# Moving two portions of an attention product from one step of a nine-step cycle to the step before it

## The chip, the cores and the metric

The kernel runs on one core of one Trainium2 chip. The metric is the time of one execution on the device, in microseconds. Each time before is one of 3 runs, and their median is what the change is compared with.

## What is computed

Attention over 8 batches and 8 heads, 576 positions, head size 64, with scores that lie more than tau below their row's largest dropped; then a mixture of 8 experts with one expert for each token. Cut to what matters:

```python
scores = scale * np.matmul(q, k.transpose(0, 1, 3, 2))
thresh = np.max(scores, axis=-1, keepdims=True) - tau
scores = np.where(scores >= thresh, scores, -1000000000.0)
attn = np.exp(scores - np.max(scores, axis=-1, keepdims=True))
attn = attn / (np.sum(attn, axis=-1, keepdims=True) + 1e-09)
x = np.matmul(attn, v)            # then tokens x (heads * head_dim)
e_idx = np.argmax(x @ w_gate, axis=1)
h = np.maximum(x[mask] @ w1[e], 0.0)
out[mask] = gate_w[mask, None] * eom[mask, e, None] * (h @ w2[e])
```

## The kernel before, in words

The attention comes first and takes about half of the span; the experts follow. The order of the instructions on TensorE (PE), VectorE (DVE), ScalarE (ACT) and GpSimd (POOL) is the order in which the code issues them. Only the DMA queue of SyncE (SP) gets its order from a scheduler.

A **unit** u is one head of two batches, which lie on the two halves of the 128 partitions; there are 32 units. Two units make a **pair** m, 16 pairs in all (0 to 15), and a pair is worked off in nine **steps** s = 0 to 8. `Attention.at` says what a step's scores are: steps 0 to 3 the four 128-row tiles of the even unit, step 4 the 64 remaining rows of both units, steps 5 to 8 the four tiles of the odd unit. The loop of `Attention.run` counts steps as g = 9 m + s, and a tile goes through it in three steps:

- In step g, `scores` multiplies q and k on TensorE into two PSUM buffers named `ps` (line L142), one for each batch. Their pool `ps_s` (L62) has two buffers in all, so the scores of the next step can be written only where this step's have been read. VectorE reads them with one operation for each batch (L153), which writes scaled scores `s` and their smallest value. ScalarE takes the exponential into `p` (`exps`, L171).
- In step g + 1, `masks` (L183, VectorE) multiplies `p` by the mask in two operations. In VectorE's queue the two masks of the tile before stand behind the two score operations of the tile now.
- In step g + 2, TensorE transposes `p`: the 64 last columns by `remainder` (L206), into a corner of the PSUM buffers `pa` or `pr`, or into fresh ones (`spots` chooses), and the rest by `blocks` (L238) into `pt`. ScalarE copies both to SBUF (L212, L241, L244), into `PTa` (the first 256 rows) and `PTb` (the last 320).

The product with the values, `av_units`, is done when a unit's tiles are transposed. It is a generator of nine **portions**: four with `PTa` into `pa`, one for the last 64 keys, and four with `PTb` into `pr` (all L252). One of the last four is two matmuls of 320 columns, which the profile shows as 4 records. After the fifth and the ninth portion the result is to be copied to `X` by ScalarE (L264 and L271); `close` issues that copy. The table `AV` (L28) says for each step which unit's portions are issued and how many, with the unit counted from 2 m. In `run` they come between the step's scores and its transposes. In step 4 (`SPLIT`) ScalarE's two exponentials stand one ahead of the transposes' corner copies and one behind.

In steps 1 and 5 (`ROWS`) `x_rows` (L306) turns a finished `X` into rows of tokens and router logits, through fresh `pr` and `pa`; in step 5 that is the odd unit of the pair before, whose product the changed entries of `AV` issue. The pairs 5 to 15 also carry operations of the router on VectorE, GpSimd and TensorE.

Of the kernel before, what the change touches and what calls it, by code (L numbers as in the profile page):

```python
# [20 lines left out]
class Attention:  # L21
# [3 lines left out]
    LB = 3  # L25
    VB = 4
    WARM = {0: 4, 1: 2}
    AV = {0: (-2, 2), 2: (-1, 5), 3: (-1, 2), 4: (-1, 2), 6: (0, 3), 7: (0, 2), 8: (0, 2)}  # L28
    SPLIT = (0, 4, 7)
    ROWS = {1: -2, 5: -1}  # L30
    LOGITS = {3: -2, 7: -1}
# [304 lines left out]
    def run(self, hooks):  # L336
# [4 lines left out]
        for g in range(G + self.TAIL):  # L341
# [36 lines left out]
            if not soon:  # L378
                self.exps(g, st, pr, (0,) if split else (0, 1))
            if s in self.AV:  # L380
                du, n = self.AV[s]
                au = 2 * m + du
# [975 lines left out]
```

## Time and profile before

| what | us |
|---|---|
| median of 3 runs | 906.42 |
| lowest and highest of them | 906.08, 906.98 |
| the profiled execution, its own time | 904.05 |
| span of that execution (first to last instruction) | 902.3 |
| busy in the span: PE, DVE, ACT, POOL | 891.8, 683.2, 595.6, 388.7 |

The profiled execution is 2.37 us (0.26%) below the median. A row of a timeline gives an instruction's start in microseconds from the start of the span, its duration, engine, line, operation, output and inputs, and, in brackets, how long the engine had been idle before it and what ended that. Durations overlap their successors a little on every engine, so the length of a piece of work is read here from start to start. Equal matmuls are merged into one row; the "x8" of one is its number of records, and a float32 matmul leaves two.

### The profile page before, as it was taken

The page shows a single profiled execution, that of the slowest core. Times are in us where ns is not written, and L with a number is a line of the kernel's source. Part 1 is how long each engine was busy: PE and PEld are TensorE (multiplying, and loading weights), DVE is VectorE, ACT ScalarE, POOL GpSimd, SP SyncE. Part 2 cuts the span into 40 slices and gives each one's busy share as a digit, 9 for nine tenths or more (in the row PEclk, how much of TensorE's full clock was granted, in tenths as well). Part 3 has the DMA queues.
Part 4 walks back from the last instruction along what each step waited for, and adds up shares of the span by engine and source line. Part 5 has one row for each costly group of instructions (what it writes and reads, how often), then busy time and mean ns, then how long its engine had stood idle before and what let it go on. Part 6 is the DMA issues. An engine that isn't in the chain of part 4 may idle for free. (4 is left out here: it accounts for less than half of the span.)

```text
span 902.3 us, 22172 instructions
## 1 busy us (share of the span) xinstructions
PE 891.8 (99%) x8345; PEld 680.5 (75%) x8345; DVE 683.2 (76%) x1704; ACT 595.6 (66%) x1159; POOL 388.7 (43%) x673
## 2 busy tenths in 40 slices
PE   8999999999999999999999999999999999999996
PEld 4666666666666666666678899888998888998885
DVE  7999999999999999999977775656556446456631
ACT  6899989999899998999974443335435335345521
POOL 4456656667866677668756710202102101112001
PEclk9999999999999999999999999999999999999999
DMA  5287421222512224254226993437646436647301
GB/s 173 93 270 235 142 87 45 85 75 79 168 44 86 73 82 165 93 170 147 96 74 204 315 293 96 152 100 241 198 143 200 162 119 213 205 128 248 114 13 45
DMA packets 70117, 127.88 MB, mean 142 GB/s; under 512 B 6408, under 2 KB 33288, under 8 KB 70009
## 3 DMA queue, kind: packets, MB, share of 16 engines
q1 hardware_dynamic: 63465, 106.03, 37.1%
q0 software_dynamic: 6544, 20.42, 5.9%
q8 instruction: 66, 1.08, 0.5%
q14 instruction: 42, 0.34, 0.1%
HBM read 95.26 MB, written 31.86 MB: 141 GB/s over the span
## 5 line engine op out<-in xcount | busy, mean ns | idle before, releaser
L171 ACT ACTIVATE p<-s,mn 128x576 f32<-128x576 f32 x288 | 215.7, 797 | 32.5 <-DVE s L153 32.5
L183 DVE SCALAR_TENSOR_TENSOR p<-s,thr,p 128x576 f32<-128x576 f32 x288 | 228.0, 828 | 3.0 <-POOL thr L160 2.8
L153 DVE TENSOR_SCALAR_CACHE_REDUCE s<-ps 128x576 f32<-128x576 f32 x288 | 206.1, 751 | 16.9 <-PE ps L142 16.5
L849 POOL DMA_INDIRECT out_dram<-yo,kid x39 | 46.4, 1189 | 323.0 <-DVE yo L848 216.7
L142 PE MATMUL ps<-qk 64*128 64x288 f32 (+1 forms) x1280 | 182.2, 419 | 0.0
L1053 ACT ACTIVATE hh<-ph 128x256 fp32r<-128x256 f32 (+7 forms) x103 | 48.7, 473 | 182.6 <-PE ph L1051 182.5
L160 POOL TENSOR_SCALAR thr<-mn,tau_sb 128x2 f32<-128x2 f32 x144 | 98.6, 685 | 129.8 <-DVE s L153 126.8
L1051 PE MATMUL ph<-xh,w1h 128*128 128x256 f32 (+7 forms) x412 | 136.7, 332 | 0.0
L1051 PE MATMUL ph<-xh,w1l 128*128 128x256 f32 (+7 forms) x412 | 133.5, 325 | 0.0
L1054 DVE SCALAR_TENSOR_TENSOR hl<-ph,hh 128x256 fp32r<-128x256 f32 (+7 forms) x103 | 54.4, 529 | 103.9 <-ACT hh L1053 103.7
L1051 PE MATMUL ph<-xl,w1h 128*128 128x256 f32 (+7 forms) x412 | 132.3, 326 | 0.0
L142 PEld LDWEIGHTS ps<-qk 64*128 64x128 f32 (+1 forms) x1280 | 108.3, 177 | 17.6 <-DVE s L153 2.8
L252 PE MATMUL pr<-PTb,vld 128*64 128x320 f32 (+1 forms) x640 | 107.2, 447 | 0.0
L238 PE MATMUL pt<-ident,p 64*128 64x64 f32 x2288 | 95.1, 223 | 0.3
L252 PE MATMUL pa<-PTa,vld 128*64 128x256 f32 (+1 forms) x640 | 84.6, 391 | 0.0
L1071 PE MATMUL py<-w2h,hh 128*128 128x512 f32 (+3 forms) x213 | 84.2, 395 | 0.0
L1072 PE MATMUL py<-w2l,hh 128*128 128x512 f32 (+3 forms) x213 | 84.0, 394 | 0.0
L1073 PE MATMUL py<-w2h,hl 128*128 128x512 f32 (+3 forms) x213 | 84.0, 394 | 0.0
L238 PEld LDWEIGHTS pt<-ident,p 64*128 64x128 f32 x2288 | 82.5, 138 | 0.8 <-ACT PTa L241 0.5
L1051 PEld LDWEIGHTS ph<-xh,w1h 128*128 128x128 f32 x412 | 77.4, 188 | 7.3
L1051 PEld LDWEIGHTS ph<-xl,w1h 128*128 128x128 f32 x412 | 77.0, 188 | 5.8
L1051 PEld LDWEIGHTS ph<-xh,w1l 128*128 128x128 f32 x412 | 77.5, 188 | 4.3
(206 smaller groups left out, 1636.9 us busy)
## 6 DMA issues: line engine op xcount, KB each, us to landing
r<-in_moe_w_dram SPq DMA_DIRECT2D x104, 512.0 KB, 3.9
qk<-in_qkv_dram SPq DMA_DIRECT2D x31, 608.0 KB, 3.9
xs<-zrow SPq DMA_DIRECT2D x40, 257.0 KB, 4.3
vld<-in_qkv_dram SPq DMA_DIRECT2D x32, 320.0 KB, 3.9
xg<-xs SPq DMA_DIRECT2D x4, 771.0 KB, 6.2
xg<-xs SPq DMA_DIRECT2D x6, 514.0 KB, 4.5
xg<-xs SPq DMA_DIRECT2D x3, 1028.0 KB, 8.3
xg<-xs SPq DMA_DIRECT2D x6, 128.5 KB, 8.3
```

Source lines behind the costliest of these rows:

```text
L142: nc.tensor.matmul(ps[a][rows, o : o + HS], q[pp, t * P : t * P + w], k[pp, k0 : k0 + HS], start=True, stop=True)
L153: nc.vector.tensor_scalar(s, ps[a][:, c0 : c0 + S], SC, None, op0=ALU.mult, op1=ALU.min, accum_out=mn[:, a : a + 1])
L160: self.router.gate = nc.gpsimd.tensor_scalar(thr, mn, self.tau, None, op0=ALU.add)
L171: self.nc.scalar.activation(e, ss[a], AF.Exp, bias=mn[:, a : a + 1], scale=-1.0)
L183: nc.vector.scalar_tensor_tensor(e, s, thr[:, a : a + 1], e, op0=ALU.is_le, op1=ALU.mult, accum_out=acc[:, a ^ (t > 1) : (a ^ (t > 1)) + 1])
L238: nc.tensor.transpose(pt[:, o : o + 64], p[hs[h], k0 : k0 + P], id_[hs[h], hs[h]])
L252: one = lambda out, l, r, start, stop: nc.tensor.matmul(out, l, r, start=start, stop=stop, skip_group_check=True)
L1051: nc.tensor.matmul(ph, w[:, c, fs], x[:, c, 0:N], start=(i == 0), stop=(i == 11))
L1054: nc.vector.scalar_tensor_tensor(hl[:, 0:N], ph, 0.0, hh[:, 0:N], op0=ALU.max, op1=ALU.subtract)
L1071: nc.tensor.matmul(Y, hh[:, ts], wh, start=(f == 0), stop=False)
L1072: nc.tensor.matmul(Y, hh[:, ts], wl, start=False, stop=False)
L1073: nc.tensor.matmul(Y, hl[:, ts], wh, start=False, stop=(f == 7))
```

## The change

The entry of step 3 goes from 2 portions to 4, and the entry of step 4 is taken out. Nothing else in the code is touched.

```diff
-    AV = {0: (-2, 2), 2: (-1, 5), 3: (-1, 2), 4: (-1, 2), 6: (0, 3), 7: (0, 2), 8: (0, 2)}
+    AV = {0: (-2, 2), 2: (-1, 5), 3: (-1, 4), 6: (0, 3), 7: (0, 2), 8: (0, 2)}
```

The product of a pair's odd unit is done in steps 2 to 4 of the next pair, so the change moves instructions in pairs 1 to 15; in pair 0 these steps have no products. Behind pair 15 the entries also serve unit 31, but no scores stand between them there, and TensorE's order is the same with both tables.

On TensorE, steps 3 and 4 of a pair without router work, before (`ps` scores, `pr<-PTb` products, `ident` transposes):

```order
L142 MATMUL ps<-qk 128x288 x4
L252 MATMUL pr<-PTb,vld 64x320 x4
L206 MATMUL pa<-ident,p 128x64
L206 MATMUL pr<-ident,p 128x64
L238 MATMUL pt<-ident,p 128x64 x16
L142 MATMUL ps<-qk 64x288 x8
L252 MATMUL pr<-PTb,vld 64x320 x4
L206 MATMUL pa<-ident,p 128x64
L206 MATMUL pr<-ident,p 128x64
L238 MATMUL pt<-ident,p 128x64 x16
L142 MATMUL ps<-qk 128x288 x4
```

and the same two steps with the change:

```order
L142 MATMUL ps<-qk 128x288 x4
L252 MATMUL pr<-PTb,vld 64x320 x8
L206 MATMUL pa<-ident,p 128x64
L206 MATMUL pr<-ident,p 128x64
L238 MATMUL pt<-ident,p 128x64 x16
L142 MATMUL ps<-qk 64x288 x8
L206 MATMUL pa<-ident,p 128x64
L206 MATMUL pr<-ident,p 128x64
L238 MATMUL pt<-ident,p 128x64 x16
L142 MATMUL ps<-qk 128x288 x4
```

Four matmuls of 320 columns went from between the scores and the transposes of step 4 to the same place of step 3. In step 4 the transposes now follow the scores directly, and their corner is a fresh `pr`.

On ScalarE, the same steps before (`X` is the copy of the product; the first four rows belong to step 3, the others to step 4):

```order
L171 ACTIVATE p<-s,mn 128x576 x2
L212 COPY PTa<-pa 128x64
L212 COPY PTa<-pr 128x64
L241 COPY PTa<-pt 128x8x128
L171 ACTIVATE p<-s,mn 128x576
L271 COPY X_215<-pr 128x320
L212 COPY PTb<-pa 128x64
```

and with the change:

```order
L171 ACTIVATE p<-s,mn 128x576 x2
L271 COPY X_215<-pr 128x320
L212 COPY PTa<-pa 128x64
L212 COPY PTa<-pr 128x64
L241 COPY PTa<-pt 128x8x128
L171 ACTIVATE p<-s,mn 128x576
L212 COPY PTb<-pa 128x64
```

The copy of the finished product moved with its last portion, from step 4 to step 3. VectorE's and GpSimd's orders are the same as before. On SP the loads of q and k and of v, which alternated, now mostly stand in twos:

```order
L96 DMA qk<-in_qkv_dram 128x1216 x2
L101 DMA vld<-in_qkv_dram 128x640 x2
```

so a load of q and k can stand behind a load of v that it stood ahead of.

## Rows read from the trace of the kernel before

**Rows 1.** Stretches from:to, with length, busy time (instructions) by engine, clock, DMA.

```profile
60.00:115.60 55.60, 55.60 (x726) 36.45 (x724) 52.42 (x148) 50.89 (x109) 33.52 (x52) 1.00 0.62 202
...
470.00:880.00 410.00, 410.00 (x2423) 362.85 (x2423) 238.63 (x450) 174.34 (x275) 80.67 (x92) 1.00 0.54 174
```

**Rows 2.** Timeline of TensorE, pair 3, steps 3 to 6: start, us, instructions.

```profile
96.46 1.19 PE L142 MATMUL ps<-qk 64*128 64x288 f32 x8
97.58 1.30 PE L252 MATMUL pr<-PTb,vld 128*64 128x320 f32 x8
...
99.51 1.20 PE L142 MATMUL ps<-qk 64*64 64x288 f32 x16
100.64 1.30 PE L252 MATMUL pr<-PTb,vld 128*64 128x320 f32 x8
101.86 0.27 PE L206 MATMUL pa<-ident,p 64*128 64x64 f32 x1
...
102.48 1.19 PE L142 MATMUL ps<-qk 64*128 64x288 f32 x8
103.50 0.23 PE L306 MATMUL pa<-wx,X 64*128 64x80 f32 x1
...
105.14 1.30 PE L142 MATMUL ps<-qk 64*128 64x288 f32 x8
106.36 1.51 PE L252 MATMUL pa<-PTa,vld 128*64 128x256 f32 x12
```

**Rows 3.** Timeline of VectorE, pair 3, steps 2 to 8, and of step 0 after.

```profile
93.45 0.75 DVE L153 TENSOR_SCALAR_CACHE_REDUCE s<-ps 128x576 f32<-128x576 f32 x1
...
97.68 0.76 DVE L153 TENSOR_SCALAR_CACHE_REDUCE s<-ps 128x576 f32<-128x576 f32 x1 [1.18 <-PE ps L142]
...
100.78 0.76 DVE L153 TENSOR_SCALAR_CACHE_REDUCE s<-ps 128x576 f32<-128x576 f32 x1 [0.18 <-PE ps L142]
...
103.70 0.76 DVE L153 TENSOR_SCALAR_CACHE_REDUCE s<-ps 128x576 f32<-128x576 f32 x1
...
104.39 0.75 DVE L153 TENSOR_SCALAR_CACHE_REDUCE s<-ps 128x576 f32<-128x576 f32 x1
...
106.54 0.75 DVE L153 TENSOR_SCALAR_CACHE_REDUCE s<-ps 128x576 f32<-128x576 f32 x1
...
109.64 0.76 DVE L153 TENSOR_SCALAR_CACHE_REDUCE s<-ps 128x576 f32<-128x576 f32 x1 [0.17 <-PE ps L142]
...
115.61 0.76 DVE L153 TENSOR_SCALAR_CACHE_REDUCE s<-ps 128x576 f32<-128x576 f32 x1
```

**Rows 4.** Timeline of VectorE, pair 0, steps 3 to 5, which have no products.

```profile
14.18 0.75 DVE L153 TENSOR_SCALAR_CACHE_REDUCE s<-ps 128x576 f32<-128x576 f32 x1
...
15.54 0.81 DVE L183 SCALAR_TENSOR_TENSOR p<-s,thr,p 128x576 f32<-128x576 f32 x1
...
17.02 0.75 DVE L153 TENSOR_SCALAR_CACHE_REDUCE s<-ps 128x576 f32<-128x576 f32 x1
...
19.85 0.75 DVE L153 TENSOR_SCALAR_CACHE_REDUCE s<-ps 128x576 f32<-128x576 f32 x1
```

**Rows 5.** Timeline of SyncE: the load of the q and k used first in Rows 6.

```profile
84.95 0.40 SPq L96 DMA_DIRECT2D qk<-in_qkv_dram  x1
```

**Rows 6.** Timeline of TensorE: the first scores of pair 4.

```profile
114.38 1.19 PE L142 MATMUL ps<-qk 64*128 64x288 f32 x8
```

**Rows 7.** Tile qk from 60 to 440 us: its loads to their landing.

```profile
DMA to landing us min/median/max: 3.6/3.8/6.6
```

**Rows 8.** Timeline of ScalarE, pair 3, from step 4 to step 6.

```profile
101.58 0.78 ACT L171 ACTIVATE p<-s,mn 128x576 f32<-128x576 f32 x1 [0.52 <-DVE s L153]
102.27 0.41 ACT L271 COPY X<-pr 128x320 f32<-128x320 f32 x1
...
104.92 0.49 ACT L363 COPY xl<-pa 128x400 f32<-128x400 f32 x1 [0.44 <-PE pa L206]
...
108.15 0.24 ACT L212 COPY PTb<-pa 128x64 f32<-128x64 f32 x1
```

## The prediction

> **What bounds the kernel now.** I read the stretches first. In the undisturbed part of the attention (60 to 115.6 us) TensorE is shown busy all the time and VectorE for 52.42 of 55.60 us; among the experts TensorE is busy all the time and VectorE for 238.63 of 410 us [rows 1]. So the experts follow TensorE's own work, which the change leaves as it is, and what the attention loses or gains moves the end by as much. In the attention two engines are close to full, and which one sets the time must be read step by step.
>
> For that I took the timelines of one cycle, pair 3. On TensorE step 3 lasts from 96.46 to 99.51, 3.05 us, and step 4 to 102.48, 2.97 us; step 5 then lasts 2.66 us [rows 2]. On VectorE I take the starts of each step's first score operation: 93.45, 97.68, 100.78, 103.70, 106.54 for steps 2 to 6 [rows 3]. Steps 2 to 5 thus last 4.23, 3.10, 2.92 and 2.84 us. Ahead of step 3 VectorE waits 1.18 us for scores, because step 2 has five portions; ahead of step 4 it waits 0.18 us [rows 3]. So TensorE paces steps 2 and 3.
>
> What VectorE needs for a step by itself is seen in pair 0, whose steps 3 and 4 have no products: from first score operation to first score operation 17.02 - 14.18 = 2.84 and 19.85 - 17.02 = 2.83 us. Two score operations take 15.54 - 14.18 = 1.36 us of that, and two masks the other 1.48 [rows 4]. Step 5 of pair 3 is at this floor; step 4 is 0.08 above it. A cycle lasts the sum of its steps, each at the slower of the two engines, so long as neither can run ahead.
>
> **Can one run ahead?** Hardly. VectorE's score operations of step 4 need TensorE's scores of step 4, which stand behind all products of step 3. VectorE cannot fill the wait with masks, since its masks of the next tile stand behind those score operations in its queue. TensorE cannot run ahead either, because the two `ps` buffers hold one step's scores: those of step 5 go where VectorE has read those of step 4. So what a long step loses on VectorE, a short step on TensorE does not give back.
>
> **The change part by part.**
>
> Step 3 gains two portions. In step 4 they take 101.86 - 100.64 = 1.22 us [rows 2], and in step 3 they stand between scores and transposes as there. TensorE's step 3 becomes 3.05 + 1.22 = 4.27 us, and VectorE's interval 3.10 + 1.22 = 4.32 us. VectorE's wait ahead of step 4 grows from 0.18 to about 1.4 us. Nothing hides it: +1.22.
>
> Step 4 loses them. TensorE's own work in it falls to 2.97 - 1.22 = 1.75 us. But its scores reach VectorE 100.78 - 99.51 = 1.27 us after the step begins [rows 2, 3], and from there VectorE needs its 2.84 us to the next first score operation [rows 4]. The interval goes from 2.92 to 2.84: -0.08. On TensorE the wait appears at the scores of step 5. They are ready to start 1.75 us into step 4, and the first `ps` is free at 1.27 + 0.76 = 2.03 us, the second at about 1.27 + 0.69 + 0.75 = 2.71 us (103.70 and 104.39 give the 0.69) [rows 3]. About 1 us of idle time or stretched scores replaces the products.
>
> Does TensorE keep a lead afterwards? Step 5 is at VectorE's floor already. The scores of step 6 wait for the second `ps` in the kernel before too: they start at 105.14, when the second score operation of step 5 ends (104.39 + 0.75), and take 106.36 - 105.14 = 1.22 us, against 97.58 - 96.46 = 1.12 in step 3 [rows 2, 3]. An earlier step 5 on TensorE can take out those 0.10 us and no more. I set this gain to zero, the value of the kernel before, and keep 0.10 for the range.
>
> The copy of `X` moves from step 4 to step 3 on ScalarE. Ahead of the exponential of step 4 ScalarE was idle for 0.52 us [rows 8], and step 3 gets 1.22 us longer, so the copy of 0.41 us is covered; without that cover it would cost at most itself. The fresh `pr` of step 4's corner needs that copy done. It comes right behind the last portion, more than a step's scores ahead of its use: nothing.
>
> The loads that change places on SP: q and k for pair 4 were issued at 84.95 [rows 5], a load lands within 6.6 us at most [rows 7], and the first scores with them start at 114.38 [rows 6]. That leaves 114.38 - 84.95 - 6.6 = 22.8 us for a load of v ahead in the queue: nothing. Without that cover, the price would be the 3.8 us of a landing at each late load.
>
> The sum: 1.22 - 0.08 = +1.14 us for a pair, in 15 pairs: **+17.1 us**. With the 0.10 of step 6 it is 1.04 x 15 = 15.6; where step 4 is not shortened at all, 1.22 x 15 = 18.3. Pairs with router work have longer steps 4 on VectorE that do not shrink, which goes towards the upper end. The profiled execution would go from 904.05 to 921.2. It lies 2.37 us under the median, so against the median of 906.42 the forecast is **923.5 us**, with 922.0 to 924.7 from these bounds.
>
> **The rivals.**
>
> *TensorE's work alone sets the time.* For it: TensorE is never shown idle [rows 1]. If it were bound by itself, 1.22 us would only change places, and step 4 would save the change from scores to products. That can be priced: scores that rows of `X` follow take 103.50 - 102.48 = 1.02 us, those that products follow 1.12 [rows 2], so 0.10 us for that change and up to 0.20 if the change back goes too. The middle, 0.15 x 15 = 2.25, gives 904.2 us: faster. It decides if the scores of step 5 start within about 1.75 us of those of step 4. Against it: the `ps` buffers, and step 6's scores, which wait for VectorE even now. The Trainium skill, TensorEngine Tiling (Array Packing), section Key Properties, has the rule that changing the tiling mode drains TensorE. By that rule alone each pair would drain once less and the change would be a gain; the 0.10 us agrees with it in direction. The forecast's mechanism outweighs it. Chance 0.05: 0.03 for faster, 0.02 for no difference.
>
> *Half of it comes back in steps 6 to 8.* From 106.54 to 109.64 is 3.10 us, and the two steps from there to 115.61 take 5.97 [rows 3]; against the floor of 2.84 that is 0.26 + 0.29 = 0.55 us. If TensorE drew a lead out of its short step, those would shrink to the floor: 1.14 - 0.55 = 0.59, times 15 = 8.9, so 915.3 us. Against it: the lead is lost at step 6's `ps`. Chance 0.08.
>
> *ScalarE becomes the late one in steps 4 and 5.* From 101.58 to 108.15 it has 6.57 us with 0.44 idle, less about 0.30 for the copy that leaves: 5.83 us of work against 2 x 2.84 = 5.68 for VectorE [rows 8]. Lateness of 0.15, or up to 0.59 if the wait of 0.44 for TensorE stays, would hold up VectorE's masks. With the middle, 0.37 x 15 = 5.6 on top, 929.1 us. Against it: ScalarE enters step 4 early, out of a long step 3. Chance 0.07.
>
> **How the numbers follow.** The forecast has 0.80, the rivals 0.05, 0.08 and 0.07. A measurement of this kernel tells about 0.2% (1.8 us) from no change; the forecast and the last two rivals lie above that: slower 0.95, same 0.02, faster 0.03. The range takes the forecast's bounds, the router pairs, and the nearer parts of the second and third rivals: 919.5 to 927.5 us.
>
> **What would show it.** In the changed profile VectorE's wait for scores ahead of step 4 should be about 1.4 us, the interval from step 3 to step 4 about 4.3 and the next 2.84; VectorE's waits for `ps` in the undisturbed pairs should about double; step 5's first score matmul should start about 2 us after step 4's, not 1.75; from step 2 to the next pair's step 0 pair 3 should take 22.16 (93.45 to 115.61 before [rows 3]) plus 1.1 us; and the experts should only be shifted. The forecast is wrong if the interval of step 4 is well under 2.84, if steps 6 to 8 shrink towards 2.84, or if VectorE waits for ScalarE in step 5.

## The result, and the profile after

The changed kernel takes 920.01 us (median of 4 runs, 919.73 to 920.94) against 906.70 us for the kernel before (median of 4 runs, 906.08 to 907.16) on the same chip. The ratio is 1.0147 with a 95% interval of 1.0135 to 1.0159: slower by 13.3 us, with 12.2 to 14.4 inside the interval. The forecast was 923.5 us, 17.1 above the median before, in a range of 919.5 to 927.5. The direction and the range held, the range by 0.5 us at its lower end; the size was too large by some 3.8 us.

The profiled execution of the changed kernel took 919.91 us, with a span of 918.2. First the page's rows for TensorE as a whole (busy us, share, instructions) and for VectorE's score operations (busy us, mean ns, then the idle time ahead of them and what ended it). The score operations before:

```profile
L153 DVE TENSOR_SCALAR_CACHE_REDUCE s<-ps 128x576 f32<-128x576 f32 x288 | 206.1, 751 | 16.9 <-PE ps L142 16.5
```

TensorE and the score operations after:

```profile
PE 903.1 (98%) x8345; PEld 684.6 (75%) x8345; DVE 682.5 (74%) x1704; ACT 597.2 (65%) x1159; POOL 387.7 (42%) x673
...
L153 DVE TENSOR_SCALAR_CACHE_REDUCE s<-ps 128x576 f32<-128x576 f32 x288 | 206.1, 751 | 33.1 <-PE ps L142 29.4
```

The score operations are as long as before, 206.1 us for 288. What grew is VectorE's wait for scores, from 16.5 to 29.4 us. TensorE's busy share goes from 99% to 98% only, although it waits more, as the next views show.

The stretches of after that answer to [rows 1] (length, busy time and instructions of PE, PEld, DVE, ACT and POOL, clock, share and GB/s of DMA):

```profile
60.00:118.00 58.00, 57.71 (x728) 37.62 (x726) 52.66 (x150) 51.67 (x109) 33.60 (x52) 1.00 0.61 197
485.00:895.00 410.00, 409.71 (x2422) 362.46 (x2421) 238.25 (x449) 174.54 (x276) 79.94 (x93) 1.00 0.53 174
```

The experts take as much TensorE and VectorE time as before. From their first matmul (464.42 us before, 479.95 after) to the end of the span it is 437.9 us before and 438.2 after, so the loss lies in the attention and is carried to the end whole.

TensorE in pair 3 of the changed kernel, steps 3 to 6, the answer to [rows 2]:

```profile
97.94 1.19 PE L142 MATMUL ps<-qk 64*128 64x288 f32 x8
99.06 2.37 PE L252 MATMUL pr<-PTb,vld 128*64 128x320 f32 x16
101.36 0.27 PE L206 MATMUL pa<-ident,p 64*128 64x64 f32 x1
...
102.06 1.20 PE L142 MATMUL ps<-qk 64*64 64x288 f32 x16
103.19 0.27 PE L206 MATMUL pa<-ident,p 64*128 64x64 f32 x1
...
104.16 1.67 PE L142 MATMUL ps<-qk 64*128 64x288 f32 x7
...
105.67 0.40 PE L142 MATMUL ps<-qk 64*128 64x288 f32 x1
...
107.35 0.46 PE L142 MATMUL ps<-qk 64*128 64x288 f32 x1
...
108.84 1.52 PE L252 MATMUL pa<-PTa,vld 128*64 128x256 f32 x12
...
110.89 1.19 PE L142 MATMUL ps<-qk 64*128 64x288 f32 x8
```

Step 3 lasts from 97.94 to 102.06, 4.12 us instead of 3.05. Its four portions take 101.36 - 99.06 = 2.30 us. Step 4 lasts until 104.16, 2.10 us; its transposes follow its scores directly. Then the scores of step 5 are drawn out: their eight records begin over 105.67 - 104.16 = 1.51 us, where in step 3 the products behind the scores could begin 1.12 us after the first of them.

VectorE in the same pair, first score operations of steps 2 to 7 and of the next pair's step 0 (of step 4 the second one too), the answer to [rows 3]:

```profile
94.94 0.75 DVE L153 TENSOR_SCALAR_CACHE_REDUCE s<-ps 128x576 f32<-128x576 f32 x1
...
99.16 0.76 DVE L153 TENSOR_SCALAR_CACHE_REDUCE s<-ps 128x576 f32<-128x576 f32 x1 [1.18 <-PE ps L142]
...
103.34 0.76 DVE L153 TENSOR_SCALAR_CACHE_REDUCE s<-ps 128x576 f32<-128x576 f32 x1 [1.26 <-PE ps L142]
...
104.02 0.75 DVE L153 TENSOR_SCALAR_CACHE_REDUCE s<-ps 128x576 f32<-128x576 f32 x1
...
106.18 0.75 DVE L153 TENSOR_SCALAR_CACHE_REDUCE s<-ps 128x576 f32<-128x576 f32 x1
...
109.02 0.75 DVE L153 TENSOR_SCALAR_CACHE_REDUCE s<-ps 128x576 f32<-128x576 f32 x1
...
112.11 0.76 DVE L153 TENSOR_SCALAR_CACHE_REDUCE s<-ps 128x576 f32<-128x576 f32 x1 [0.17 <-PE ps L142]
...
118.08 0.76 DVE L153 TENSOR_SCALAR_CACHE_REDUCE s<-ps 128x576 f32<-128x576 f32 x1
```

Steps 2 to 6 last 4.22, 4.18, 2.84, 2.84 and 3.09 us, against 4.23, 3.10, 2.92, 2.84 and 3.10 before. The wait ahead of step 4 is 1.26 us instead of 0.18. From there to step 6 (103.34 to 109.02) VectorE is shown without idle time: steps 4 and 5 are its own work. From step 2 to the next pair it is 118.08 - 94.94 = 23.14 us against 22.16, and whole pairs without router work (1 to 4) take 28.95 instead of 27.95. So a pair loses **1.00 us**, all of it in steps 3 and 4: +1.08 and -0.08.

TensorE's weight loads in step 5, with their wait in brackets:

```profile
104.16 0.29 PEld L142 LDWEIGHTS ps<-qk 64*128 64x128 f32 x2 [0.28 <-DVE s L153]
104.84 0.54 PEld L142 LDWEIGHTS ps<-qk 64*128 64x128 f32 x5 [0.38 <-DVE s L153]
```

They wait twice for VectorE's score operations of step 4, once for each `ps` buffer: the first is read until 103.34 + 0.76 = 104.10, the second until 104.02 + 0.75 = 104.77. This wait stands in no such row of pair 3 before.

ScalarE from step 3 to step 5, the answer to [rows 8]:

```profile
101.68 0.43 ACT L271 COPY X<-pr 128x320 f32<-128x320 f32 x1 [0.26 <-PE pr L206]
...
104.14 0.78 ACT L171 ACTIVATE p<-s,mn 128x576 f32<-128x576 f32 x1 [0.89 <-DVE s L153]
...
107.31 0.49 ACT L363 COPY xl<-pa 128x400 f32<-128x400 f32 x1 [0.61 <-PE pa L206]
```

The copy of `X` (L271) is now in step 3. Ahead of the exponential of step 4 ScalarE is idle for 0.89 us, 0.52 before: it is early there.

Over pairs 1 to 15, from the first score operation of pair 1 to that of the last step, the changed kernel takes 437.0 us. In the first profile of before that is 421.0, in the profile of its copy below 422.5. Fifteen times 1.00 would be 15.0; the difference to the copy is 14.5. Of the pairs with router work, 5, 8, 9 and 12 lose less than 1.00 against the copy (0.93, 0.80, 0.90 and 0.82 us), and 6, 7, 10, 11 and 13 lose more (1.07 to 1.10). Pairs 5 to 13 together fall short of nine times 1.00 by only 0.13 us; the rest lies in pairs 14 and 15 (0.58 and 1.05), which also differ between executions of one kernel.

### The profile page after: what moved, and what is told of

The parts are those of the page before. It is cut to its first block, busy times and chain, and to the rows that moved or that the text cites. A ratio compares the mean times of both kernels' runs of the same rounds, so it can differ in the third digit from the quotient of the medians.

```text
span 918.2 us, 22185 instructions
## 1 busy us (share of the span) xinstructions
PE 903.1 (98%) x8345; PEld 684.6 (75%) x8345; DVE 682.5 (74%) x1704; ACT 597.2 (65%) x1159; POOL 387.7 (42%) x673
## 3 DMA queue, kind: packets, MB, share of 16 engines
q8 instruction: 66, 1.08, 0.5%
## 5 line engine op out<-in xcount | busy, mean ns | idle before, releaser
L153 DVE TENSOR_SCALAR_CACHE_REDUCE s<-ps 128x576 f32<-128x576 f32 x288 | 206.1, 751 | 33.1 <-PE ps L142 29.4
L142 PE MATMUL ps<-qk 64*128 64x288 f32 (+1 forms) x1280 | 194.5, 421 | 3.1 <-DVE pr L662 1.4
L142 PEld LDWEIGHTS ps<-qk 64*128 64x128 f32 (+1 forms) x1280 | 111.1, 177 | 31.2 <-DVE s L153 12.7
L252 PE MATMUL pr<-PTb,vld 128*64 128x320 f32 (+1 forms) x640 | 103.8, 444 | 0.0
L238 PE MATMUL pt<-ident,p 64*128 64x64 f32 x2288 | 100.0, 224 | 1.5 <-ACT PTb L244 1.0
L238 PEld LDWEIGHTS pt<-ident,p 64*128 64x128 f32 x2288 | 86.1, 138 | 2.5 <-ACT PTb L244 1.3
```

What stands on the lines that cost most here:

```text
L142: nc.tensor.matmul(ps[a][rows, o : o + HS], q[pp, t * P : t * P + w], k[pp, k0 : k0 + HS], start=True, stop=True)
L153: nc.vector.tensor_scalar(s, ps[a][:, c0 : c0 + S], SC, None, op0=ALU.mult, op1=ALU.min, accum_out=mn[:, a : a + 1])
L238: nc.tensor.transpose(pt[:, o : o + 64], p[hs[h], k0 : k0 + P], id_[hs[h], hs[h]])
L252: one = lambda out, l, r, start, stop: nc.tensor.matmul(out, l, r, start=start, stop=stop, skip_group_check=True)
```

## Experiments

Three questions were open behind these views: whether the loss grows with the portions moved or comes all at once with the last one; whether TensorE really has idle time in steps 4 and 5; and which of two limits holds those steps, VectorE's 2.84 us of work or the `ps` buffers. The first three kernels below ran on one chip with the kernel before at 905.78 us, the others on chips where it took 905.77 and 906.25.

**Half of the change.**

```diff
-    AV = {..., 3: (-1, 2), 4: (-1, 2), ...}
+    AV = {..., 3: (-1, 3), 4: (-1, 1), ...}
```

> Step 3 issues 3 portions and step 4 one: half of the change. The copy of X stays in step 4, the corner of step 4's transposes stays in pr, and the products still stand between step 4's scores and its transposes. Theory (each portion moved lengthens the step that TensorE paces, and VectorE's floor of 2.84 us keeps step 4 from getting shorter): in the changed kernel's trace two portions more cost step 3 of pair 3 1.08 us, so one costs 0.54; step 4 falls by 0.08 at most; 0.46 us for a pair, 7 us in 15 pairs, so half of the change's loss, 913 to 914 us; VectorE's interval from step 3 to step 4 3.64 us, from step 4 to step 5 2.84. Rival 1 (TensorE's work alone sets the time): 906 to 907. Rival 2 (the loss comes from the moved copy of X, the fresh pr or the transposes directly behind the scores, all of which come with the last portion only): 906 to 907.5 here, the whole loss with the fourth portion.

Measured: 912.19 us, ratio 1.0063 (1.0044 to 1.0083), 4.0 to 7.5 us slower and a little under the 913 to 914 expected. Pairs 1 to 4 take 28.42 us, 0.47 more than before. VectorE's first score operations of steps 3, 4 and 5 in pair 3:

```profile
98.93 0.76 DVE L153 TENSOR_SCALAR_CACHE_REDUCE s<-ps 128x576 f32<-128x576 f32 x1 [1.19 <-PE ps L142]
...
102.58 0.76 DVE L153 TENSOR_SCALAR_CACHE_REDUCE s<-ps 128x576 f32<-128x576 f32 x1 [0.72 <-PE ps L142]
...
105.42 0.75 DVE L153 TENSOR_SCALAR_CACHE_REDUCE s<-ps 128x576 f32<-128x576 f32 x1
```

The intervals are 3.65 and 2.84 us: +0.55 and -0.08. The loss in a pair is about half of the change's 1.00, with half of the portions. It does not hang on the moved copy, the fresh `pr` or the transposes directly behind the scores, which this kernel doesn't have; and TensorE's work alone, which is the same, does not set the time.

**The mirror: all four portions in step 4.**

```diff
-    AV = {..., 3: (-1, 2), 4: (-1, 2), ...}
+    AV = {..., 4: (-1, 4), ...}
```

> The mirror of the change: step 3 has no portion, step 4 all four. Theory: step 3 cannot get under VectorE's 2.84 us, so it goes from 3.10 to 2.84, and step 4 goes from 2.92 to about 3.75 to 4.0 (1.08 us of products more, less what TensorE is ahead in step 3): +0.6 to +0.8 us for a pair, 9 to 12 us in all, 916 to 919 us, a little under the change's loss because step 3 lay 0.26 above the floor and step 4 only 0.08. Rival 1 (TensorE's work alone): 906 to 907. Rival 2 (the loss belongs to step 3, or to the moved copy of X): no loss here, 905 to 907.

Measured: 917.52 us, ratio 1.0143 (1.0105 to 1.0181). Pairs 1 to 4 take 28.68 to 28.69 us, 0.74 more. VectorE's first score operations of steps 3 to 6 in pair 3:

```profile
99.66 0.76 DVE L153 TENSOR_SCALAR_CACHE_REDUCE s<-ps 128x576 f32<-128x576 f32 x1 [1.19 <-PE pr L206]
...
102.50 0.75 DVE L153 TENSOR_SCALAR_CACHE_REDUCE s<-ps 128x576 f32<-128x576 f32 x1
...
106.41 0.76 DVE L153 TENSOR_SCALAR_CACHE_REDUCE s<-ps 128x576 f32<-128x576 f32 x1 [1.00 <-PE ps L142]
...
109.26 0.75 DVE L153 TENSOR_SCALAR_CACHE_REDUCE s<-ps 128x576 f32<-128x576 f32 x1
```

Step 3 fell to 2.84 us and no further, step 4 rose to 3.91. So the loss is not tied to step 3; uneven steps cost the same either way, less the 0.26 us by which step 3 lay above 2.84.

**A copy of the kernel before**, run and profiled again because the two first profiles lie further apart than the medians.

> The kernel before, unchanged, profiled again. The profiled executions of before and after lie 15.9 us apart, the medians 13.3: the first profile of before (904.05 us) lies 2.0 us under the fastest of its runs shown. If that execution was an exception, this one's span is 904 to 905.5 us and its profiled time 906 to 907, and the pairs 1 to 4 still take 27.95 us each, so that the rest lies elsewhere. If the profile differs from the timed runs as a rule, this one's span is again 902 to 903 us.

Measured: 905.88 us, ratio 1.0002 (0.9979 to 1.0026); profiled at 905.17 us with a span of 903.5, which lies between what the two readings expected. Pairs 1 to 4 take 27.95 to 27.96 us again. Most of the difference to the first profile is in pairs 14 and 15: 28.97 and 25.38 us up to the last step here, 28.05 and 24.96 there. The changed kernel's profile has 29.55 and 26.43 there, so the first profile of before had these two pairs some 1.3 us shorter than its copy, for a reason that no run here settles. The forecast took differences from pairs 0 and 3, so it didn't suffer.

**Six matmuls in step 4 that nothing needs**, in the kernel before and in the changed one.

```diff
+            if s == 4 and 0 < m < 16:
+                fw = self.ident.bitcast(BF16)
+                fp = self.ps_t.tile([P, 1024], F32, name="pt")
+                for _ in range(6):
+                    nc.tensor.matmul(fp[:, 0:256], fw[:, 0:P], fw, start=True, stop=True)
             if s in self.AV:
```

> The kernel before with six matmuls of 256 columns in bfloat16 put behind the scores of step 4 in pairs 1 to 15; their result is used by nothing. Both theory and rivals: TensorE has no room in step 4 of this kernel, so they cost their whole time, 0.65 to 1.0 us for a pair, and the time goes to 916 to 922 us. This measures their price.

> The same six matmuls at the same place of the changed kernel. Theory (TensorE waits there for VectorE, about 0.9 us between the shortened step 4 and the stretched scores of step 5): they cost 0 to 0.2 us for a pair, so 920 to 923 us, and the two kernels with the filling lie within some 4 us of each other. Rival (TensorE has no room: the change costs time on TensorE itself, by its longer row of products or by changes of tile shape): they cost what they cost in the kernel before, 930 us or more, and the distance of 13.3 us stays.

Measured: 923.88 us with the table of before, ratio 1.0206 (1.0189 to 1.0223), some 18 us more; 920.93 us with the changed table, ratio to the kernel before 1.0169 (1.0152 to 1.0186), where the change alone had 1.0147. Step 4 of pair 3 on TensorE, in the kernel before with the filling:

```profile
102.22 1.20 PE L142 MATMUL ps<-qk 64*64 64x288 f32 x16
103.83 0.81 PE L384 MATMUL pt<-ident 128*128 128x256 bf16 x6 [0.40 <-ACT PTa L241]
104.57 1.30 PE L252 MATMUL pr<-PTb,vld 128*64 128x320 f32 x8
```

and in the changed kernel with it:

```profile
103.20 1.20 PE L142 MATMUL ps<-qk 64*64 64x288 f32 x16
104.44 0.82 PE L384 MATMUL pt<-ident 128*128 128x256 bf16 x6
105.19 0.27 PE L206 MATMUL pa<-ident,p 64*128 64x64 f32 x1
...
105.87 1.34 PE L142 MATMUL ps<-qk 64*128 64x288 f32 x8
```

With the table of before a pair goes from 27.95 to 29.17 us: 1.22, of which the matmuls are 104.57 - 103.83 = 0.74, and the rest is mostly a wait of 0.40 us for `pt`. That was more than expected, in the pair and in the whole (916 to 922 us). With the changed table the same matmuls take 105.19 - 104.44 = 0.75 us of TensorE, and pairs 1 to 4 stay at 28.94 to 28.96 us: they cost 0.00. The scores of step 5 now start 2.67 us after those of step 4 instead of 2.10, at the time the second `ps` is free, and are no longer drawn out. So TensorE has at least 0.75 us of idle time there which its busy share doesn't show. Of the pairs 5 to 13 all but one stay within 0.02 us as well; pair 7 is 1.45 us longer, all of it in its step 7, for a reason that no run here settles.

**VectorE's masks halved for one tile**, those that run in step 4, with both tables.

```diff
-            e = pr[g][:, a * self.S : a * self.S + self.S]
-            self.nc.scalar.activation(e, ss[a], AF.Exp, bias=mn[:, a : a + 1], scale=-1.0)
+            w = self.S // 2 if g % 9 == 3 and g > 9 else self.S
+            e = pr[g][:, a * self.S : a * self.S + w]
+            self.nc.scalar.activation(e, ss[a][:, 0:w], AF.Exp, bias=mn[:, a : a + 1], scale=-1.0)
...
-            e = p[:, a * S : a * S + S]
+            w = S // 2 if t == 3 and i == 0 and u > 1 else S
+            e = p[:, a * S : a * S + w]
...
-                e, s, thr[:, a : a + 1], e, op0=ALU.is_le, op1=ALU.mult, accum_out=...
+                e, s[:, 0:w], thr[:, a : a + 1], e, op0=ALU.is_le, op1=ALU.mult, accum_out=...
...
-            self.nc.gpsimd.tensor_scalar(r, self.sums[m][:, i], 1e-9, None, op0=ALU.add)
+            self.nc.gpsimd.tensor_scalar(r, self.sums[m][:, i], 1.0, None, op0=ALU.add)
```

> The kernel before, with the exponentials and the masks of one tile (the fourth tile of the even unit, in pairs 1 to 15) done on the first half of the columns only, and 1.0 added to the sums in place of 1e-9; the second half of p keeps older values, so those rows and the weights differ from the reference, and tokens can go to other experts. VectorE's work in step 4 falls from 2.84 to about 2.15 us. Theory: TensorE paces step 4 here, so the interval from step 4 to step 5 stays near 2.9 and the pairs 1 to 4 stay within 0.1 us of 27.95.

> The changed kernel with the same tile halved. Theory (VectorE's work holds step 4 at 2.84 us): the interval from step 4 to step 5 falls to 2.1 to 2.4, the ps buffers then being the limit, and the pairs 1 to 4 are only 0.4 to 0.7 us longer than with the table of before and the same halving, where they are 1.00 us longer without it. Rival 1 (the loss lies on TensorE or ScalarE, not in VectorE's floor): the difference stays at 1.00 us and the interval at 2.84. Rival 2 (the ps buffers alone hold step 5 back, whatever VectorE has to do behind its score operations): also 1.00 us.

Measured: with the table of before pairs 1 to 4 take 27.94 to 27.95 us, with the changed one 28.84 to 28.85. The whole kernels took 985.56 and 996.49 us; nearly all of what they take more comes after the attention, most likely because tokens go to other experts, so only the pairs are compared. VectorE with the changed table, pair 3, first score operations of steps 4 to 7 and the first of the halved masks:

```profile
103.24 0.76 DVE L153 TENSOR_SCALAR_CACHE_REDUCE s<-ps 128x576 f32<-128x576 f32 x1 [1.26 <-PE ps L142]
...
104.60 0.08 DVE L153 DVE_READ_ACCUMULATOR s<-ps 128x1 f32 x1
...
105.54 0.76 DVE L153 TENSOR_SCALAR_CACHE_REDUCE s<-ps 128x576 f32<-128x576 f32 x1
...
108.47 0.76 DVE L153 TENSOR_SCALAR_CACHE_REDUCE s<-ps 128x576 f32<-128x576 f32 x1
...
111.83 0.76 DVE L153 TENSOR_SCALAR_CACHE_REDUCE s<-ps 128x576 f32<-128x576 f32 x1 [0.25 <-PE ps L142]
```

and TensorE's scores of steps 4, 5 and 6 (first rows):

```profile
101.96 1.20 PE L142 MATMUL ps<-qk 64*64 64x288 f32 x16
...
104.06 1.67 PE L142 MATMUL ps<-qk 64*128 64x288 f32 x7
...
107.25 0.46 PE L142 MATMUL ps<-qk 64*128 64x288 f32 x1
```

VectorE's step 4 did fall, from 2.84 to 2.30 us, but steps 5 and 6 rose to 2.93 and 3.36 us, and the pair got only 0.10 us shorter. The distance between the tables is 0.90 us; 0.4 to 0.7 was expected. TensorE's scores of steps 5 and 6 start 2.10 and 5.29 us after those of step 4, just as without the halving. So VectorE's 2.84 us is a limit, and a second one lies only 0.10 us behind it: with the first out of the way, TensorE, held up by the `ps` buffers at step 5, keeps most of the loss.

**VectorE's score operations halved in step 4** instead, with both tables. This is nearly the same saving on VectorE, but it frees the `ps` buffers earlier.

```diff
+            w = S // 2 if t == self.NB and u > 1 else S
+            if w < S:
+                nc.gpsimd.memset(s[:, w:S], 0.0)
             nc.vector.tensor_scalar(
-                s, ps[a][:, c0 : c0 + S], SC, None, op0=ALU.mult, op1=ALU.min, accum_out=mn[:, a : a + 1]
+                s[:, 0:w], ps[a][:, c0 : c0 + w], SC, None, op0=ALU.mult, op1=ALU.min, accum_out=mn[:, a : a + 1]
```

> The kernel before, with the score operations of step 4 reading the first half of their columns only, in pairs 1 to 15; GpSimd fills the other half of s with zeros, so half of the keys drop out for those rows, the output differs from the reference's and tokens can go to other experts. VectorE's work in step 4 falls by about as much as with the halved masks, and the ps buffers are free earlier, by some 0.35 us (the first) and 0.7 us (the second). Both theories: TensorE paces step 4 here, the pairs 1 to 4 stay within 0.1 us of 27.95 us.

> The changed kernel with the same halving. The halved masks took VectorE's step 4 from 2.84 to 2.30 us and shortened the pair by 0.10 only, so the first theory (VectorE's 2.84 us as the floor of step 4) does not hold the loss. New theory: TensorE's scores of step 5 wait for VectorE to read the ps buffers in step 4, once for each buffer, and this time TensorE does not get back. Then earlier free buffers give most of it back: step 5's scores start about 1.8 us after step 4's, not 2.1, and are not stretched much; the pairs 1 to 4 take 28.1 to 28.4 us, 0.15 to 0.45 above the table of before with the same halving. Rival (it is VectorE's amount of work around step 4, and halving either kind gives the same 0.10): 28.85 us, and 0.90 above.

Measured: with the table of before pairs 1 to 4 take 27.95 to 28.03 us, with the changed one 28.34 to 28.43: 0.31 to 0.40 apart, within what was expected. (The whole kernels took 990.05 and 994.95 us, again with most of the excess after the attention.) VectorE with the changed table, pair 3, first score operations of steps 4 to 7:

```profile
102.01 0.46 DVE L156 TENSOR_SCALAR_CACHE_REDUCE s<-ps 128x288 f32<-128x288 f32 x1 [1.25 <-PE ps L142]
...
104.26 0.75 DVE L156 TENSOR_SCALAR_CACHE_REDUCE s<-ps 128x576 f32<-128x576 f32 x1
...
107.09 0.74 DVE L156 TENSOR_SCALAR_CACHE_REDUCE s<-ps 128x576 f32<-128x576 f32 x1
...
110.19 0.76 DVE L156 TENSOR_SCALAR_CACHE_REDUCE s<-ps 128x576 f32<-128x576 f32 x1 [0.18 <-PE ps L142]
```

and TensorE's scores of steps 4 and 5:

```profile
100.74 1.20 PE L142 MATMUL ps<-qk 64*64 64x288 f32 x16
...
102.53 1.37 PE L142 MATMUL ps<-qk 64*128 64x288 f32 x7
```

VectorE's step 4 is 2.25 us, as with the halved masks, and yet the pair is 0.5 us shorter than there: 28.34 us in pair 3 instead of 28.85. TensorE's scores of step 5 start 1.79 us after those of step 4, which is TensorE's own work, and steps 5 and 6 on VectorE stay at 2.83 and 3.10. Two changes of nearly the same size on VectorE thus give 0.10 and 0.60 us; what tells them apart is when VectorE has read `ps`. With the buffers free earlier VectorE has no idle time from 102.01 to 107.09 again, and the pair gains all that VectorE saves. So both limits count in the changed kernel, VectorE's work first and the buffers 0.10 us behind it. Two things are not separated. No run frees the buffers earlier at VectorE's full 2.84 us; by the rows of the changed kernel, where VectorE has no idle time in steps 4 and 5, that alone should give nothing. And ScalarE also gets its input earlier with shorter score operations. Its idle time of 0.89 us in step 4 speaks against its being late, but no run here takes that away alone.

## Why the prediction was right, and where its sizes were off

*The experts follow the attention's end*: right, 437.9 and 438.2 us.

*TensorE paces steps 2 and 3, and VectorE can't use the wait*: right. The wait ahead of step 4 rose by 1.08 us and nothing hid it.

*Step 3 pays +1.22*: the term that was mis-sized. It measured +1.08. The forecast took the time of a group of two portions for two portions more. The runs show a group of two at 1.22 us in [rows 2], of four at 2.30, and one portion more at 0.55 (3.65 - 3.10 on VectorE with three portions): about 0.54 for a portion and 0.14 once for the group. Step 3 had a group before the change and has one after it, so the fixed part was already paid there, and the forecast counted it a second time. The rival's price of 0.10 to 0.20 for a change between scores and products is of the same size, but it belongs to another place: in step 4 the scores take 1.13 us whether products follow (100.64 - 99.51) or transposes (103.19 - 102.06), so nothing was saved there. The Trainium skill, TensorEngine Tiling (Array Packing), section Key Properties, says that changing the tiling mode drains TensorE; a cost once for each group is what it would look like, but no run here separates the drain from the rest of that 0.14.

*Step 4 gives back 0.08*: right in size, 2.92 to 2.84. Its reason holds in the trace: VectorE works through steps 4 and 5 without idle time. But the forecast named two limits, VectorE's 2.84 us and the two `ps` buffers, and priced the step by the first alone. The halved masks show that without the first the second still costs 0.90 of the 1.00 us, and the halved score operations, which ease both, give 0.60 back.

*TensorE keeps no lead*: right. Before, step 6 of pair 3 ends on TensorE with the scores of step 7:

```profile
108.42 1.19 PE L142 MATMUL ps<-qk 64*128 64x288 f32 x8
```

Steps 4 to 6 take 2.10 + 3.19 + 3.54 = 8.83 us on TensorE now, against 108.42 - 99.51 = 8.91 before, although two portions are gone from them; steps 6 to 8 did not shrink (3.09 and 5.97 us on VectorE, against 3.10 and 5.97). The scores of step 5 began 2.10 us after those of step 4, where about 2 was forecast.

*The copy of `X`, the fresh `pr`, the loads on SP at nothing*: the first two are borne out by half the change, which moves neither and pays its share. Of the loads no run took the order alone; that pairs 1 to 4 lose 1.00 us in steps 3 and 4 alone leaves no place for them there.

*Pairs with router work lose more*: right for some, wrong for others. In pairs 6, 7, 10, 11 and 13 step 4 does not shrink, as forecast, and they lose 1.07 to 1.10 us. Pairs 5, 8, 9 and 12 lose 0.80 to 0.93 us, because their step 3 grows by only 0.90 to 0.94: VectorE came late to it with operations of the router (intervals of 2.81 to 2.90 us before), and that lateness is now hidden in the wait ahead of step 4. Over pairs 5 to 13 the two nearly cancel.

The sum by measured terms is (1.08 - 0.08) x 15 = 15.0; less 0.1 in pairs 5 to 13 and 0.4 in pairs 14 and 15 it is the 14.5 between the profiles. The medians have 13.3, with 12.2 to 14.4 in the interval; that last difference of about 1 us no run explains. That the range held has some luck in it: the bounds of the sum, 922.0 to 924.7, miss 920.01, and the range reached down to 919.5 only because it took in the nearer part of a rival that did not come true. Of the rivals, TensorE alone and the part that comes back in steps 6 to 8 fell by these views, and ScalarE became earlier, not later. None of the tables tried beats the kernel before.

## What to carry to other kernels

Where one engine fills a buffer that another must read before the next step may be filled, the two run in step, and moving work from one step to the next costs what the longer step gains, less what the shorter one lay above its other limit, however busy the engine is shown. Two limits can lie close together, and then taking one away shows only the distance to the other. Look for what frees the buffer, not only for the reader's total work: nearly the same saving on VectorE was worth six times as much in the operations that free `ps`. Price added instructions as a slope and a fixed part, from two groups of different length.

## What the runs showed that was not expected

- Six matmuls of 0.75 us cost a pair 0.00 us in the changed kernel and 1.22 us in the kernel before, at the same place; there a wait of 0.40 us for `pt` is part of it.
- TensorE's busy share falls only from 99% (891.8 of 902.3 us) to 98% (903.1 of 918.2), although the filling shows 0.75 us and more of idle time in pairs 1 to 6 and 8 to 13. The drawn-out scores, and the weight loads' waits of 0.28 and 0.38 us in pair 3, show it better.
- Two executions of the same kernel differ by 1.3 us in pairs 14 and 15 alone.
